# A fused top-k attention and gated feed-forward kernel: weight conversion through one PSUM bank, one rounding moved from ScalarE to GpSimd, GpSimd's budget of tasks 2.25 instead of 2.0

## The chip, the cores and the metric

The kernel runs on one core of a Trainium2 chip. The metric is the device time of one execution in microseconds. Before the change the median of three runs is 1152.47 us (1152.42 to 1154.94).

## The reference

For 8 batches and 8 heads, 576 rows of queries, keys and values of 64 columns: scores, all but the 32 largest of each row masked out, softmax, times the values. The heads side by side are the input x (8, 576, 512) of a feed-forward part: expansion to 1024 columns, relu, a convolution of three taps along the rows, a sigmoid gate, contraction to 512 columns.

```python
scores = scale * np.matmul(q, k.transpose(0, 1, 3, 2))
kth = np.partition(scores, -top_k, axis=-1)[..., -top_k:-top_k + 1]
scores = np.where(scores >= kth, scores, -1000000000.0)
attn = np.exp(scores - max); attn = attn / (sum + 1e-09)
x = np.matmul(attn, v)                       # heads side by side
h = np.maximum(x @ w_in, 0.0)
conv_out += conv_w[k] * hp[:, k:k + S, :]    # k = 0, 1, 2
gate = 1.0 / (1.0 + np.exp(-conv_out))
return (h * gate @ w_out).astype(np.float32)
```

The three weights arrive as 64-bit floats (NumPy's square roots, by which they are scaled, make them so), q, k and v as 32-bit floats.

## The kernel before

The attention is cut into 288 tiles of 128 rows by 576 scores: 32 pairs of heads, nine tiles each. One call of `iteration(it)` issues one step of a software pipeline, in which some eight tiles are in different states. The order in which each engine gets its instructions is the order of this code; the engines themselves run free and wait for each other by semaphores. In an iteration:

- TensorE transposes the masked weights of an old tile, multiplies those of a still older one by the values, computes the scores of a new tile, and in between does feed-forward matmuls, as many as a budget (`FEED`) allows.
- ScalarE, in its order: relu of an expansion, the rounding of gated activations where one is due (L531), the signs ("side", L268), the copy of the scores out of PSUM ("rows", L228), other copies; then the exponential of the scores into PSUM (L280), which waits until the weighing has read the one before, then the tanh of a gate (L465), then its share of a weight block (L155 to L157).
- VectorE: in a loop of seven places, a maximum of a seventh of a tile's row ("cand", L235) in each place, with steps of the search for the 32nd largest of another tile between them, the maximum of the flipped row (L283) in the third place and the selection of the threshold ("hot", L287) in the fifth. Behind the loop come gates (L473), and as the last the weighing (L293): mask times exponential, with the row's sum.
- GpSimd: its share of a weight block (L166 to L172), then the flip ("z", L273: scores times their sides) of one tile, and before or behind it tasks of the feed-forward part from a queue.

The queue of GpSimd, `pool_tasks`, holds planned costs and the earliest iteration of each task. In each iteration `state.pool` gets `POOL_BUDGET`, less 1.5 for a converted block, with deficits carried over. Tasks are issued while more than 0.2 is left. The flip goes in front of the next task as soon as less than `FLIP_AT` = 1.5 is left, and at the end of the iteration at the latest. Tasks are the two halves of a convolution (L439, L448), the three steps of a normalisation (L372 to L374), a gate now and then, and the subtraction (L535) of a rounded activation.

The weight conversion (`class Convert`) is a pipeline of its own over the first iterations: 33 blocks (a small one of the convolution, 16 of 128x256 of each matrix), one an iteration. VectorE masks the exponent field out of a block's high word (`split`, L150, L151), ScalarE makes powers of two and mantissas of it (`act`, L155 to L157), VectorE puts the sign on the power (`sign`, L161), GpSimd multiplies and splits the product into a rounded part and the rest (`pool`). The masks stand in the first places of VectorE's loop, the sign behind the loop. All temporaries lie in SBUF. Feed-forward work starts when the input weights are converted and the first batch's attention is there.

`Contract.split` readies half of a contraction: the gated activations g are rounded to the matmul's format (hi) on ScalarE at once, and the rest g - hi (lo) is a task of GpSimd. Behind the last attention tile (`state.it > NT + 4`) VectorE makes the rest instead.

Of the kernel before, what the change touches and what calls it, by code (L numbers as in the profile page):

```python
# [13 lines left out]
BF16 = mybir.dt.bfloat16  # L14
U16 = mybir.dt.uint16
U32 = mybir.dt.uint32
AF = mybir.ActivationFunctionType
# [21 lines left out]
CB = 1  # L39
BELOW_AT = 2  # L40
NATB = 2
POOL_BUDGET = 2.0
PE_CAP = 1.6
FEED = 1.42
CONV_COST = 1.5
# [18 lines left out]
def attend_and_feed(ctx: ExitStack, tc: tile.TileContext, q, k, v, weights, out, shared, finish=None):  # L64
# [53 lines left out]
    def bank(name):  # L118
        return ps.tile([P, BANK], F32, name=name, tag=name, bufs=1)
# [6 lines left out]
    class Convert:  # L126
# [5 lines left out]
        def load(self):  # L132
            i = Convert.count
            Convert.count += 1
            if not scratch:
                scratch.append(moe.tile([P, 4 * SPB, WB], F32, name="scratch", tag="split"))
            self.at = i % SPB * 4
            tag = ("x_hi", "x_lo")[i % 2]
            self.raw = xp.tile([P, self.src.shape[-1], 2], U32, name="raw64", tag=tag)[0:self.n]
            nc.sync.dma_start(out=self.raw.rearrange("a c t -> a (c t)"), in_=self.src.bitcast(U32))  # L140
# [2 lines left out]
            return scratch[0][0:self.n, self.at + i, 0:self.raw.shape[1]]  # L143

        def split(self):
            exponent, self.mantissa, self.rest = (self.tmp(i) for i in range(3))
            n = exponent.shape[1]
            self.field, self.power = exponent.bitcast(U16)[:, 0:n], exponent.bitcast(BF16)[:, n:2 * n]
            self.top = self.raw.rearrange("a c t -> a (c t)").bitcast(U16).rearrange("a (c t) -> a c t", t=4)[:, :, 3]
            yield lambda: nc.vector.tensor_scalar(self.field, self.top, 0x7FF0, None, ALU.bitwise_and)  # L150
            yield lambda: nc.vector.tensor_scalar(self.mantissa.bitcast(U32), self.raw[:, :, 1], 0xFFFFF, 0x100000,  # L151
                                                  ALU.bitwise_and, ALU.bitwise_or)

        def act(self):
            nc.scalar.activation(out=self.power, in_=self.field, func=AF.Exp, scale=math.log(2.0) / 16, bias=offset)  # L155
            nc.scalar.activation(out=self.mantissa, in_=self.mantissa.bitcast(U32), func=AF.Copy, scale=2.0 ** -20)
            nc.scalar.activation(out=self.rest, in_=self.raw[:, :, 0], func=AF.Copy, scale=2.0 ** -52)  # L157

        def sign(self):
            power = self.power.bitcast(U16)  # L160
            yield lambda: nc.vector.scalar_tensor_tensor(out=power, in0=self.top, scalar=0x8000, in1=power,  # L161
                                                         op0=ALU.bitwise_and, op1=ALU.bitwise_or)

        def pool(self):
            x = self.mantissa
# [330 lines left out]
    class Contract:  # L496
# [11 lines left out]
        def split(self):  # L508
# [18 lines left out]
            state.split += 1  # L527
            state.splits += 0 if late else 1
            state.late_splits += 1 if late else 0
            for a, z, src in srcs:  # L530
                nc.scalar.copy(out=self.hi[:, :, a:z], in_=src)  # L531

            def rest(engine):
                for a, z, src in srcs:
# [1 line left out]
                self.ready = True  # L536
                unready.remove(self)

            if state.it > NT + 4:
                rest(nc.vector)  # L540
            else:
                pool_tasks.append((state.it + 1, 1.3, lambda: rest(nc.gpsimd)))

        def room(self):
# [169 lines left out]
    def iteration(it):  # L714
# [45 lines left out]
        for i in range(max(7, len(a_ops), len(b_ops))):  # L760
            if i < len(a_ops):
                a_ops[i]()
            for op in c_first[i:i + 1]:
                op()
            if tD is not None and not exact:
                if i == BELOW_AT:
                    below(tD)
                if i == BELOW_AT + 2:
                    select(tD)
            if i < len(b_ops):  # L770
                b_ops[i]()
        for op in c_last:
            op()
        while gates:
            gates.popleft().gate()
        recs, rec_next = rec_next, []
# [189 lines left out]
```

## Time and profile before

| | |
|---|---|
| median of 3 runs | 1152.47 us |
| the profiled execution | 1155.28 us |
| its span, first to last instruction | 1153.4 us |
| mean granted TensorE clock | 0.963 of full |
| TensorE busy (matmuls) | 1035.3 us |
| VectorE busy | 1064.5 us |
| ScalarE busy | 996.5 us |
| GpSimd busy | 895.6 us |

Busy times are unions of instruction spans on an engine; DVE is VectorE, ACT is ScalarE, POOL is GpSimd, PE is TensorE and PEld its weight loads. The pipelines of TensorE and VectorE overlap neighbouring instructions a little, so the sums of durations are larger than the busy time. Durations and stretches come from the profiled execution.

### The profile page before, as it was taken

What the parts mean: (1) busy time and instruction counts of PE and PEld (TensorE: products, weight loads), DVE (VectorE), ACT (ScalarE), POOL (GpSimd) and SP (SyncE); (2) the same over time, 40 slices, a digit from 0 to 9 for tenths busy, and PEclk for the clock granted to TensorE, in tenths of its full rate; (3) what the DMA queues carried; (4) which work ended last, traced back from release to release, by engine and by line L of the source; (5) the groups of instructions that cost most, each with busy time, mean ns of one, the idle gap of its engine ahead of it and who ended that gap; (6) DMA issues with size and microseconds to landing.
All of it is one profiled execution on the core that took longest, in us unless ns stands there. A gap on an engine that the chain in (4) does not pass through costs nothing.

```text
span 1153.4 us, 27267 instructions
## 1 busy us (share of the span) xinstructions
PE 1035.3 (90%) x7970; PEld 767.3 (67%) x7970; DVE 1064.5 (92%) x5834; ACT 996.5 (86%) x2343; POOL 895.6 (78%) x1078
## 2 busy tenths in 40 slices
PE   3665676788999999999999999999999999999997
PEld 1443444566767776777777767777777677777896
DVE  7999999999999999999999999999999999998651
ACT  5777868899999999999999999999999999998442
POOL 6788864688979888898978887987978897898300
PEclk9967659999999999999999999999999999999999
DMA  7221101111111111111111112121211011110001
GB/s 242 79 68 41 46 17 40 46 38 44 55 54 56 56 46 65 46 55 56 49 38 44 56 45 64 47 64 46 64 55 56 24 38 59 55 33 21 31 28 40
DMA packets 51694, 60.75 MB, mean 53 GB/s; under 512 B 9776, under 2 KB 30544, under 8 KB 51536
## 3 DMA queue, kind: packets, MB, share of 16 engines
q1 hardware_dynamic: 51536, 58.91, 16.0%
q8 instruction: 66, 1.08, 0.4%
q14 instruction: 92, 0.75, 0.2%
HBM read 49.31 MB, written 9.58 MB: 51 GB/s over the span
## 4 chain that ended last, share of the span: by engine, by line
DVE 45%; PE 42%; ACT 11%; issue 1%; DMA 0%; SPq 0%; POOL 0%; ACTq 0%; POOLq 0%
DVE cand L235 13%; DVE e L293 9%; PE mc L554 9%; PE me L404 8%; DVE z L283 7%; PE s_ps L337 6%; PE s_ps L219 5%; PE pt L306 5%; DVE cand L257 3%; ACT weights_ps L280 2%; DVE scratch L161 2%; DVE rows L255 2%; PE s_ps L222 2%; DVE hot L287 2%; PE weights_ps L554 2%; PE s_ps L214 2%
## 5 line engine op out<-in xcount | busy, mean ns | idle before, releaser
L273 POOL TENSOR_TENSOR z<-rows,side 128x579 f32<-128x579 f32 x288 | 347.4, 1206 | 143.0 <-ACT side L268 122.5
L235 DVE MAX8 cand<-rows 128x8 f32<-128x82 f32 (+1 forms) x2016 | 451.0, 238 | 0.0
L280 ACT ACTIVATE weights_ps<-rows,z 128x576 f32<-128x576 f32 x288 | 219.8, 763 | 42.4 <-DVE e L293 31.5
L293 DVE SCALAR_TENSOR_TENSOR e<-rows,kth,weights_ps 128x576 f32<-128x576 f32 x288 | 230.1, 799 | 0.3
L268 ACT ACTIVATE side<-rows 128x576 bf16<-128x576 f32 x288 | 224.2, 778 | 0.8 <-DVE rows L255 0.5
L404 PE MATMUL me<-x_hi,wi 128*128 128x322 f32 (+1 forms) x928 | 218.6, 308 | 1.2 <-ACT g L418 1.2
L283 DVE MAX8 z<-z 128x8 f32<-128x576 f32 x288 | 213.7, 742 | 0.0
L228 ACT COPY rows<-s_ps 128x576 f32<-128x576 f32 x288 | 183.0, 635 | 33.7 <-PE s_ps L340 20.3
L219 PE MATMUL s_ps<-k,q 64*128 64x512 f32 x512 | 155.1, 684 | 59.6 <-ACT xt L348 44.9
L306 PE MATMUL pt<-ident,e 128*128 128x128 f32 x1152 | 191.8, 292 | 8.9 <-DVE e L293 8.9
L337 PE MATMUL s_ps<-pT,vn 128*64 128x128 f32 (+1 forms) x2560 | 171.2, 279 | 17.7 <-ACT rows L228 17.7
L554 PE MATMUL mc<-wo,split 128*128 128x512 f32 x684 | 186.5, 406 | 0.0
L337 PEld LDWEIGHTS s_ps<-pT,vn 128*64 128x64 f32 x2560 | 134.3, 143 | 54.7 <-ACT rows L228 28.0
L306 PEld LDWEIGHTS pt<-ident,e 128*128 128x128 f32 x1152 | 135.3, 148 | 35.3 <-issue 20.1
L404 PEld LDWEIGHTS me<-x_hi,wi 128*128 128x128 f32 x928 | 157.1, 189 | 2.4 <-ACT g L418 2.1
L311 ACT COPY pT<-pt 128x512 f32<-128x512 f32 x256 | 152.0, 594 | 3.4 <-PE pt L306 3.2
L404 PE MATMUL me<-x_lo,wi 128*128 128x258 f32 (+1 forms) x464 | 138.5, 299 | 0.0
L554 PEld LDWEIGHTS mc<-wo,split 128*128 128x128 f32 x684 | 120.1, 189 | 19.6 <-issue 0.2
L437 POOL TENSOR_SCALAR t<-g,cr 128x256 f32<-128x256 f32 (+1 forms) x222 | 113.6, 512 | 0.0
L222 PEld LDWEIGHTS s_ps<-k,q 128*128 128x128 f32 x256 | 40.9, 201 | 105.6 <-issue 105.6
L255 DVE MAX8 rows<-cand 128x8 f32<-128x21 f32 x576 | 108.9, 189 | 0.2 <-issue 0.2
L219 PEld LDWEIGHTS s_ps<-k,q 64*128 64x128 f32 x512 | 40.6, 194 | 91.2 <-ACT xt L348 58.8
(121 smaller groups left out, 1865.6 us busy)
## 6 DMA issues: line engine op xcount, KB each, us to landing
k<-in_k_dram SPq DMA_DIRECT2D x32, 352.0 KB
q<-in_q_dram SPq DMA_DIRECT2D x32, 288.0 KB
vn<-in_v_main_dram SPq DMA_DIRECT2D x32, 256.0 KB
rb<-row SPq DMA_DIRECT2D x64, 128.0 KB
out_dram<-o SPq DMA_DIRECT2D x24, 256.0 KB
raw<-in_w_in_dram SPq DMA_DIRECT2D x16, 256.0 KB
raw<-in_w_out_dram SPq DMA_DIRECT2D x16, 256.0 KB
vt<-in_v_tail_dram SPq DMA_DIRECT2D x32, 64.0 KB
```

What stands on the lines that cost most here:

```text
L219: nc.tensor.matmul(s_ps[:, 2 * h * BANK:(2 * h + 1) * BANK], lhsT=qx[d, at], rhs=kx[d, h * TAIL:h * TAIL + MAIN], start=True, stop=True)
L228: nc.scalar.copy(out=x, in_=s_ps[:, at:at + S])
L235: yield lambda c=c, at=at, n=n: nc.vector.max(out=t.cand[:, c:8 * CHUNKS:CHUNKS], in_=t.x[:, at:at + n])
L268: nc.scalar.activation(out=t.side[:, 2:S + 2], in_=t.x, func=AF.Sign, scale=-OVER, bias=t.row[:, 7:8], accum_out=t.cnt)
L273: nc.gpsimd.tensor_tensor(t.z[:, 8:S + 11], t.row[:, 6:S + 9], t.side, ALU.mult)
L280: nc.scalar.activation(out=e_ps, in_=t.x, func=AF.Exp, scale=scale, bias=t.shift)
L283: nc.vector.max(out=t.z[:, 0:8], in_=t.z[:, 10:S + 10])
L293: nc.vector.scalar_tensor_tensor(out=t.e, in0=t.x, scalar=kth[:, t.n:t.n + 1], in1=e_ps, op0=ALU.is_ge, op1=ALU.mult, accum_out=t.pc.sums[ ...
L306: nc.tensor.transpose(tp[:, i * P:(i + 1) * P], t.e[:, o + i * P:o + (i + 1) * P], ident)
L337: nc.tensor.matmul(a[r, 0:w], lhsT=st.pc.vn[:, h, i], rhs=st.pT[:, h if st.i < NI else 1 - h, i, 0:w], start=(i == 0), stop=False)
L404: nc.tensor.matmul(mm[:, 0:w], lhsT=wt, rhs=xx, start=(n == 0), stop=(n == len(ops) - 1))
L554: nc.tensor.matmul(mm[0:m], lhsT=x[:, i], rhs=wo[:, e, f], start=start, stop=stop)
```

## The change

Four things change. The exponent field and the mantissa bits of a weight block move from SBUF to two halves of one PSUM bank (that of "mc", which no contraction uses yet), in whole 4-byte words; ScalarE makes the power of two in SBUF and copies it to the field's place, one instruction more, and the sign is put on from there. The sign and the two masks of the next block go to the fifth, sixth and seventh place of VectorE's loop, the sign first. The rounding of gated activations becomes a task of GpSimd, with a planned cost of 0.65, in front of its subtraction; behind the last tile it stays on ScalarE. `POOL_BUDGET` goes from 2.0 to 2.25.

```diff
-POOL_BUDGET = 2.0
+POOL_BUDGET = 2.25
@@ Convert.load
                 scratch.append(moe.tile([P, 4 * SPB, WB], F32, name="scratch", tag="split"))
+                mc = bank("mc")
+                scratch.extend((mc[:, 0:WB], mc[:, WB:2 * WB]))
@@ Convert.split
-            exponent, self.mantissa, self.rest = (self.tmp(i) for i in range(3))
-            n = exponent.shape[1]
-            self.field, self.power = exponent.bitcast(U16)[:, 0:n], exponent.bitcast(BF16)[:, n:2 * n]
-            self.top = self.raw.rearrange("a c t -> a (c t)").bitcast(U16).rearrange("a (c t) -> a c t", t=4)[:, :, 3]
-            yield lambda: nc.vector.tensor_scalar(self.field, self.top, 0x7FF0, None, ALU.bitwise_and)
-            yield lambda: nc.vector.tensor_scalar(self.mantissa.bitcast(U32), self.raw[:, :, 1], 0xFFFFF, 0x100000,
+            self.power, self.mantissa, self.rest = (self.tmp(i) for i in range(3))
+            self.two = self.power.bitcast(BF16)[:, 0:self.power.shape[1]]
+            self.field, self.bits = (x[0:self.n, 0:self.raw.shape[1]] for x in scratch[1:])
+            self.top = self.raw[:, :, 1]
+            yield lambda: nc.vector.tensor_scalar(self.field.bitcast(U32), self.top, 0x7FF00000, None, ALU.bitwise_and)
+            yield lambda: nc.vector.tensor_scalar(self.bits.bitcast(U32), self.top, 0xFFFFF, 0x100000,
                                                   ALU.bitwise_and, ALU.bitwise_or)
@@ Convert.act
-            nc.scalar.activation(out=self.power, in_=self.field, func=AF.Exp, scale=math.log(2.0) / 16, bias=offset)
-            nc.scalar.activation(out=self.mantissa, in_=self.mantissa.bitcast(U32), func=AF.Copy, scale=2.0 ** -20)
+            nc.scalar.activation(out=self.two, in_=self.field.bitcast(U32), func=AF.Exp, scale=math.log(2.0) / 2 ** 20,
+                                 bias=offset)
+            nc.scalar.copy(out=self.field, in_=self.two)
+            nc.scalar.activation(out=self.mantissa, in_=self.bits.bitcast(U32), func=AF.Copy, scale=2.0 ** -20)
@@ Convert.sign
-            power = self.power.bitcast(U16)
-            yield lambda: nc.vector.scalar_tensor_tensor(out=power, in0=self.top, scalar=0x8000, in1=power,
-                                                         op0=ALU.bitwise_and, op1=ALU.bitwise_or)
+            yield lambda: nc.vector.scalar_tensor_tensor(out=self.power.bitcast(U32), in0=self.top, scalar=0x80000000,
+                                                         in1=self.field.bitcast(U32), op0=ALU.bitwise_and,
+                                                         op1=ALU.bitwise_or)
@@ Contract.split
-            for a, z, src in srcs:
-                nc.scalar.copy(out=self.hi[:, :, a:z], in_=src)
+            def cast():
+                for a, z, src in srcs:
+                    if state.it > NT + 4:
+                        nc.scalar.copy(out=self.hi[:, :, a:z], in_=src)
+                    else:
+                        nc.gpsimd.tensor_scalar(self.hi[:, :, a:z], src, 1.0, 0.0, ALU.mult, ALU.add)
...
-            if state.it > NT + 4:
+            if late:
+                cast()
                 rest(nc.vector)
             else:
+                pool_tasks.append((state.it + 1, 0.65, cast))
                 pool_tasks.append((state.it + 1, 1.3, lambda: rest(nc.gpsimd)))
@@ iteration
-            for op in c_first[i:i + 1]:
+            for op in (c_last + c_first)[i - 4:i - 3] if i > 3 else ():
                 op()
...
-        for op in c_last:
-            op()
         while gates:
             gates.popleft().gate()
```

## Rows read from the trace of the kernel before

**Rows 1.** The page, part 1: busy time, share of the span, instructions, by engine.

```profile
PE 1035.3 (90%) x7970; PEld 767.3 (67%) x7970; DVE 1064.5 (92%) x5834; ACT 996.5 (86%) x2343; POOL 895.6 (78%) x1078
```

**Rows 2.** Busy time by stretch: length, busy us (instructions) by engine, clock, DMA.

```profile
20.00:160.00 140.00, 84.78 (x478) 52.76 (x479) 139.79 (x620) 102.95 (x252) 115.91 (x148) 0.77 0.17 53
160.00:180.00 20.00, 16.36 (x106) 10.01 (x108) 16.70 (x102) 15.08 (x35) 10.74 (x12) 0.68 0.21 65
300.00:1000.00 700.00, 683.08 (x5511) 509.55 (x5510) 677.16 (x3937) 663.83 (x1556) 599.06 (x704) 1.00 0.16 51
```

**Rows 3.** Line 293 from 29 to 120 us: count, ns min/median/max, first and last start.

```profile
L293 DVE SCALAR_TENSOR_TENSOR e<-rows,kth,weights_ps x19: 798/801/804, 29.6 to 119.5; 128x576 f32<-128x576 f32 x19
```

**Rows 4.** Groups by line, 20 to 160 us: busy us, mean ns | idle before, releasers.

```profile
L161 DVE SCALAR_TENSOR_TENSOR scratch<-raw,scratch 128x256 uint16<-128x256 uint16 x29 | 29.5, 1018 | 0.0
L150 DVE TENSOR_SCALAR scratch<-raw 128x256 uint16<-128x256 uint16 x27 | 15.7, 582 | 0.0
L151 DVE TENSOR_SCALAR scratch<-raw 128x256 uint32<-128x256 uint32 x27 | 11.6, 429 | 0.0
```

**Rows 5.** Timeline in the head: start us, us, engine line op.

```profile
63.50 1.21 POOL L273 TENSOR_TENSOR z<-rows,side 128x579 f32<-128x579 f32 x1 [1.09 <-ACT side L268]
...
63.73 1.25 DVE L161 SCALAR_TENSOR_TENSOR scratch<-raw,scratch 128x256 uint16<-128x256 uint16 x1
...
71.15 0.27 DVE L150 TENSOR_SCALAR scratch<-raw 128x256 uint16<-128x256 uint16 x1
...
71.58 0.33 DVE L151 TENSOR_SCALAR scratch<-raw 128x256 uint32<-128x256 uint32 x1
...
72.30 0.40 ACT L156 ACTIVATE scratch<-scratch 128x256 f32<-128x256 uint32 x1
...
73.19 0.23 DVE L235 MAX8 cand<-rows 128x8 f32<-128x82 f32 x1
...
73.90 0.40 DVE L161 SCALAR_TENSOR_TENSOR scratch<-raw,scratch 128x256 uint16<-128x256 uint16 x1
```

**Rows 6.** Groups by line, whole span: gates with and without PSUM, and a PSUM write.

```profile
L473 DVE SCALAR_TENSOR_TENSOR g<-weights_ps,g 128x256 f32<-128x256 f32 x49 | 19.9, 407 | 0.0
L473 DVE SCALAR_TENSOR_TENSOR g<-t,g 128x256 f32<-128x256 f32 x8 | 3.3, 423 | 0.8 <-ACT t L465 0.8
L352 DVE TENSOR_SCALAR weights_ps<-sums 128x9 f32<-128x9 f32 x32 | 5.5, 170 | 1.1
```

**Rows 7.** Groups by line, 20 to 160 us: ScalarE’s exponential, GpSimd’s first add.

```profile
L280 ACT ACTIVATE weights_ps<-rows,z 128x576 f32<-128x576 f32 x27 | 20.2, 747 | 32.9 <-DVE e L293 27.4 <-DVE rec L353 3.9 <-DVE cand L235 1.5
L166 POOL TENSOR_TENSOR scratch<-scratch 128x256 f32<-128x256 f32 x28 | 23.9, 854 | 0.0
```

**Rows 8.** Timeline of VectorE behind the last block: two weighings.

```profile
155.15 0.80 DVE L293 SCALAR_TENSOR_TENSOR e<-rows,kth,weights_ps 128x576 f32<-128x576 f32 x1
...
175.25 0.80 DVE L293 SCALAR_TENSOR_TENSOR e<-rows,kth,weights_ps 128x576 f32<-128x576 f32 x1
```

**Rows 9.** Groups by line, 300 to 1000 us: the flip, and hot.

```profile
L273 POOL TENSOR_TENSOR z<-rows,side 128x579 f32<-128x579 f32 x201 | 242.1, 1205 | 84.3 <-ACT side L268 78.4 <-DVE rows L255 3.7 <-POOL split L535 1.0
L287 DVE SCALAR_TENSOR_TENSOR hot<-weights_ps,cnt,z 128x10 f32<-128x10 f32 x201 | 43.2, 215 | 21.1 <-ACT weights_ps L465 16.0 <-ACT weights_ps L280 4.1
```

**Rows 10.** Line 531, the roundings on ScalarE, 200 to 1050 us.

```profile
L531 ACT CAST split<-g x56: 406/622/714, 276.7 to 1046.2; 128x512 fp32r<-128x512 f32 x50, 128x256 fp32r<-128x256 f32 x6
L531 ACT CAST split<-ends x6: 391/404/434, 492.1 to 1014.0; 128x256 fp32r<-128x256 f32 x6
```

**Rows 11.** Lines 373 and 171: roundings of other tiles on GpSimd.

```profile
L373 POOL TENSOR_SCALAR x_hi<-xt x32: 661/672/844, 104.3 to 1080.2; 128x576 fp32r<-128x576 f32 x32
...
L171 POOL TENSOR_SCALAR wi<-scratch x16: 404/404/428, 12.8 to 81.3; 128x256 fp32r<-128x256 f32 x16
```

**Rows 12.** Timeline around 820 us: a flip, and the exponential that reads it.

```profile
819.54 1.20 POOL L273 TENSOR_TENSOR z<-rows,side 128x579 f32<-128x579 f32 x1
...
822.32 0.77 ACT L280 ACTIVATE weights_ps<-rows,z 128x576 f32<-128x576 f32 x1
```

## The prediction

> **What bounds the kernel now.** I read the page's busy line first: VectorE 92%, TensorE 90%, ScalarE 86%, GpSimd 78% of the span [rows 1]. Four engines that full cannot be told apart by a mean, so I split the span into stretches. From 20 to 160 us VectorE is busy 139.79 of 140 us and no other engine is over 83%: this is the head, where the weights are converted, one block to an iteration, and VectorE sets the pace. From 300 to 1000 us TensorE (97.6%) and VectorE (96.7%) are both nearly full, ScalarE stands at 95%, GpSimd at 86% [rows 2]. Behind that comes a tail of feed-forward matmuls, which is TensorE's.
>
> One weighing (L293) ends each iteration, so its starts are a ruler. Nineteen of them run from 29.6 to 119.5 us: 89.9 / 18 = 4.99 us an iteration [rows 3]. In the steady stretch there are 201 iterations in 700 us: 3.48 us each [rows 9]. So the head pays 1.5 us more an iteration, for the 27 blocks that are masked from 20 us on [rows 4], 25 of them at this full pace, and for the ramp before.
>
> What is in that 1.5 us? The three conversion operations on VectorE take 1018, 582 and 429 ns on the mean, 2.03 us together [rows 4]. These means are not work. One sign operation (L161) starts at 63.73, beside a GpSimd multiply that runs from 63.50 to 64.71, and takes 1.25 us; the same operation takes 0.40 at 73.90, and the masks (L150, L151) take 0.27 and 0.33 at 71.15 and 71.58 [rows 5]. So each often waits out a GpSimd operation that got in first. The weighing, one of whose operands lies in PSUM, never does: 798 to 804 ns over all 19 [rows 3].
>
> The Trainium skill says the like in "SBUF — State Buffer", section "Who interferes with whom": VectorE and GpSimd share one pair of SBUF ports, a lock held for a whole instruction, which a VectorE instruction wants if it has two SBUF inputs or runs in a two-port mode. The sign and the weighing agree with the first half; a mask has one input, so by that rule it must run in such a mode, which no row here shows.
>
> **The change, part by part.**
>
> *Head, VectorE.* The sign operation will have one SBUF and one PSUM input, and the masks read 4-byte words and write PSUM. If all three take what they take when nothing is in their way, an iteration loses 1.018 - 0.40 + 0.582 - 0.27 + 0.429 - 0.33 = 1.03 us: 4.99 - 1.03 = 3.96 [rows 3 to 5]. For the price of a PSUM operand the nearest row is the gate (L473) at 128x256: 407 ns with a PSUM input, 423 with all in SBUF; a nine-column tensor_scalar into PSUM takes 170 ns [rows 6], about what is left of 330 ns when 256 columns are taken off at the weighing's slope, 0.8 us for 576. So the three cost 0 to 0.2 us more than the free ones; I take 0.1: 4.06.
>
> "VectorE: DVE Perf Modes" in the Trainium skill, section "The TRN2 errata", speaks against this: a VectorE operation from PSUM has a fixed part of 120 cycles, one from SBUF of 58. For the one PSUM input of a block that is 65 ns, an estimate from that page, and 2 us over the head. The gate's two rows don't bear it out.
>
> *Head, the new wait.* The sign moves from the end of the iteration to its fifth place, and field and bits lie in one bank that ScalarE uses too, so it must wait until ScalarE has done that block's exponential, the new copy and the mantissa. That a bank is guarded as a whole is seen in "hot" (L287): it reads constants, and waits 16.0 us for a ScalarE write to other columns of their bank [rows 9]. In the iteration with the free masks ScalarE's mantissa ends at 72.30 + 0.40 = 72.70; the copy in front of it, of the same shape, adds at most 0.40, some 0.35 with the overlap: 73.05. VectorE comes to the sign behind the fifth chunk, 73.19 + 0.23, and no longer has the two masks ahead of it, -0.60: 72.82 [rows 5]. The wait is 0.2 us (0 to 0.4). Behind it in VectorE's queue stand "hot", two chunks, both masks and the weighing, and ScalarE's next exponential waits for that, so it counts whole: 4.26.
>
> *Head, the other engines.* ScalarE is busy 102.95 of 140 us, 3.67 of each 4.99, with the copy 4.05. It has the room, for it waits 32.9 us for VectorE's weighing [rows 2, 7]. GpSimd is busy 115.91 of 140, 4.13 an iteration; its first add (854 ns [rows 7]) loses a port wait of its own, so some 4.1. TensorE's granted clock is 0.77 there and 0.68 from 160 to 180 us, so part of both is at the lower level, 1.2 GHz [rows 2]. Behind the last block, with no conversion and no feed-forward matmul yet, five iterations take 175.25 - 155.15 = 20.1 us, 4.02 each [rows 8], with TensorE's late results as what holds them. So at 4.26 VectorE still sets the pace, but three others stand at 4.0 to 4.1 and their waits will not all fall together: I take 4.4, bounds 3.96 and 4.75 (the latter if each iteration pays a wait of half a microsecond). Saved: 25 x (4.99 - 4.4) = 15 us (bounds 6 and 26), and 2 (0 to 4) in the ramp. The head is a fixed number of iterations, so what it saves moves everything behind it.
>
> *Steady stretch, ScalarE.* 62 roundings (56 + 6) of 0.62 us, 0.40 for the 12 short ones, leave ScalarE between 276 and 1046 us: 36 us [rows 10]. What can come of it is bounded twice: TensorE idles 16.9 us of 700, and VectorE waits 21.1 of 700 at "hot" [rows 2, 9]. Only those waits can give, and the feed-forward matmuls have to be done whatever the iteration takes. I take 3 us, bounds 0 and 10.
>
> *Steady stretch, GpSimd.* The same rounding takes 404 ns there at 256 columns and 672 at 576 [rows 11], so 0.62 at 512: 50 x 0.62 + 12 x 0.40 = 36 us over some 770. Busy goes from 86 to about 90%, and 78.4 us of waiting for ScalarE's sides in 700 [rows 9] are there to fill. Queued behind a rounding on GpSimd stand its subtraction and that iteration's flip (L273), for which ScalarE's next exponential waits, and VectorE's max behind it. In the tightest iteration from 200 to 1050 us the flip ends at 820.74 and that exponential starts at 822.32: 1.58 us of room [rows 12]; one rounding fits. The larger budget admits 2.25 instead of 2.0 of planned cost to an iteration; what it is spent on is the same work, so it costs nothing unless flips come late. A contraction becomes ready at most an iteration later, and TensorE has expansions to put in its place. I take 0, bounds -2 and +10.
>
> *Tail.* There the rounding stays on ScalarE and the subtraction on VectorE: 0.
>
> **Sum.** -15 - 2 - 3 = -20 us on the profiled execution's 1155.28 (span 1153.4 and 1.9 around it): 1135. The median of the runs, 1152.47, is 2.8 lower: forecast 1132.
>
> **Rivals.**
> 1. The head goes to the floor of 3.96 and the freed ScalarE takes away half of the waits at "hot": -26 - 4 - 10 = -40, 1112. For it: "hot" waits for ScalarE alone. Against: three other engines stand at 4.0 to 4.1.
> 2. The bank holds the head up, ScalarE and VectorE each late behind the other, 4.75 an iteration: -6, 1146. For it: "hot" pays for sharing a bank already. The Trainium skill asks for such waits in "PSUM — Partial Sum Buffer", section "PSUM bank collisions raise a hardware error": engines are to be kept apart by bank, not by address. The row of "hot" agrees.
> 3. Slower: GpSimd sets the pace of the steady stretch. The place is the flip behind rounding and subtraction: both are admitted before it, since 2.25 - 0.65 is still over the flip's mark of 1.5. It decides once the delay exceeds the room, 1.58 us at the tightest. If 62 such groups cost the rounding's 0.6 each: 37 - 20 = +17, 1169. For it: GpSimd at 90%, and a budget that with a flip fills 3.5 us. Against: its 78.4 us of waiting, and only one rounding to two or three iterations.
> 4. It does not do what it says: masks and sign, with one operand still in SBUF, wait for the port as before: -3, 1150.
>
> **How the numbers follow.** Forecast 0.63, rival 1 0.12, rival 2 0.13, rival 3 0.06, rival 4 0.06. About 0.3%, 3.5 us, is what a measurement of this kernel can tell. Faster: 0.63 + 0.12 and 0.10 of rival 2, 0.85; same: the rest of rival 2 and rival 4, 0.09; slower: 0.06. The range for 8 in 10 leaves out rivals 3 and 4 and the far ends of 1 and 2: 1117 to 1148.
>
> **What would show it.** Right: the sign near 0.41 us in every place and both masks near 0.33, whatever GpSimd does; weighings 4.2 to 4.6 us apart in the head; the steady stretch at 3.45 to 3.5; roundings of 0.62 on GpSimd. Wrong: signs that idle over 0.5 us behind ScalarE, flips that end behind the exponential's turn, or a clock in the head that takes another course.

## The result and the profile after

The changed kernel takes 1136.76 us in the median of 4 runs (1134.84 to 1138.28) against 1153.51 in 4 runs of the kernel before on the same chip: 0.985 of it, interval 0.983 to 0.988. That is 16.8 us less; 20 were forecast, and 1132 us. The profiled execution took 1135.4 us, its span is 1133.6.

The page's busy line of the changed kernel, to be laid beside [rows 1]: VectorE 22 us less, ScalarE 12 less, GpSimd 36 more.

```profile
PE 1020.9 (90%) x7970; PEld 757.7 (67%) x7970; DVE 1042.4 (92%) x5831; ACT 984.1 (87%) x2312; POOL 931.4 (82%) x1147
```

Its stretches (length, busy us of PE, PEld, DVE, ACT and POOL with instructions, granted clock, DMA), which answer to [rows 2]: the head, the iterations right behind it, the steady stretch, and all behind the last weighing.

```profile
20.00:140.00 120.00, 73.49 (x452) 43.98 (x451) 113.12 (x590) 110.25 (x271) 104.70 (x139) 0.81 0.19 62
143.00:170.00 27.00, 18.82 (x166) 12.18 (x164) 26.74 (x163) 24.18 (x57) 19.94 (x21) 0.93 0.15 48
300.00:1000.00 700.00, 687.40 (x5568) 514.01 (x5567) 681.66 (x3958) 648.22 (x1515) 635.96 (x773) 1.00 0.17 52
1045.20:1134.00 88.80, 76.69 (x446) 65.81 (x445) 39.96 (x82) 31.55 (x72) 17.85 (x22) 0.96 0.10 32
```

In the head VectorE is no longer the only full engine: 113.1 of 120 us, with ScalarE at 110.3. In the steady stretch ScalarE went from 663.8 to 648.2 and GpSimd from 599.1 to 636.0, while TensorE and VectorE are each busy some 4 us longer in the same 700. For the stretch behind the head and the one behind the last weighing, the same two rows of the kernel before:

```profile
155.10:180.00 24.90, 19.33 (x127) 12.24 (x125) 21.53 (x127) 18.81 (x44) 15.39 (x17) 0.64 0.17 52
1063.70:1154.00 90.30, 81.69 (x491) 71.48 (x487) 41.30 (x85) 33.87 (x76) 14.40 (x17) 0.97 0.09 31
```

The ruler in the head, the weighing (now L297), which answers to [rows 3]:

```profile
L297 DVE SCALAR_TENSOR_TENSOR e<-rows,kth,weights_ps x19: 797/802/808, 28.6 to 110.5; 128x576 f32<-128x576 f32 x19
```

Nineteen weighings from 28.6 to 110.5 us: 81.9 / 18 = 4.55 us an iteration on the mean, against 4.99; 12 of the 18 take 4.45. And the three conversion operations on VectorE from 28 to 138 us, which answer to [rows 4] (busy us, mean ns, idle before and its releaser):

```profile
L164 DVE SCALAR_TENSOR_TENSOR scratch<-raw,mc 128x256 uint32<-128x256 uint32 x24 | 10.1, 422 | 6.1 <-ACT scratch L160 6.1
L152 DVE TENSOR_SCALAR mc<-raw 128x256 uint32<-128x256 uint32 x25 | 10.4, 415 | 0.0
L153 DVE TENSOR_SCALAR mc<-raw 128x256 uint32<-128x256 uint32 x25 | 10.4, 415 | 0.0
```

Every one of them has a constant duration now (the signs 420 to 423 ns, the masks 410 to 420), though every sign starts while a GpSimd operation runs, and 1.25 us in sum replace 2.03. In front of the sign (L164) stands the new wait, 6.1 us in 24 iterations, for ScalarE's mantissa (L160). One iteration of the timeline (start us, us, engine, line) shows it:

```profile
94.67 0.38 ACT L160 ACTIVATE scratch<-mc 128x256 f32<-128x256 uint32 x1
...
95.08 0.42 DVE L164 SCALAR_TENSOR_TENSOR scratch<-raw,mc 128x256 uint32<-128x256 uint32 x1 [0.19 <-ACT scratch L160]
...
95.84 0.41 DVE L152 TENSOR_SCALAR mc<-raw 128x256 uint32<-128x256 uint32 x1
...
96.32 0.41 DVE L153 TENSOR_SCALAR mc<-raw 128x256 uint32<-128x256 uint32 x1
...
96.64 0.80 DVE L297 SCALAR_TENSOR_TENSOR e<-rows,kth,weights_ps 128x576 f32<-128x576 f32 x1
```

Mantissa, 0.19 us of idle, sign, masks, and from the sign's start to the weighing's 1.56 us. The steady stretch's flip and "hot", which answer to [rows 9], and the roundings on GpSimd, which answer to [rows 10]:

```profile
L277 POOL TENSOR_TENSOR z<-rows,side 128x579 f32<-128x579 f32 x202 | 243.4, 1205 | 44.3 <-ACT side L272 37.0 <-PE pt L310 4.5 <-PE s_ps L226 2.2
...
L291 DVE SCALAR_TENSOR_TENSOR hot<-weights_ps,cnt,z 128x10 f32<-128x10 f32 x202 | 43.5, 215 | 16.7 <-ACT weights_ps L469 14.6 <-ACT weights_ps L284 1.2
```

```profile
L540 POOL TENSOR_SCALAR split<-g x57: 404/619/631, 265.2 to 1041.5; 128x512 fp32r<-128x512 f32 x51, 128x256 fp32r<-128x256 f32 x6
...
L540 POOL TENSOR_SCALAR split<-ends x6: 404/406/423, 482.1 to 989.1; 128x256 fp32r<-128x256 f32 x6
```

GpSimd's wait for sides halves, 78.4 to 37.0 us; VectorE's at "hot" goes from 21.1 to 16.7.

Where the 19.8 us of span went, with the starts of the first, 28th, 55th and last weighing as marks: up to the 28th (162.2 before, 149.6 after) 12.6 us, all in the ramp and the head; from there to the 55th (253.7 and 237.8) 3.3; from the 55th to the last (1063.7 and 1045.2) 2.6; from the last to the last matmul's end (1145.7 and 1123.9) 3.3; and the last copies and outputs took 2.0 us longer than before. The second of these need not be the kernel's: behind the head the granted clock was 0.64 in the one execution and 0.93 in the other, as the two rows show, and that differs between executions of the same instructions too (last section).

### The profile page after: what moved, and what is told of

Read it like the earlier page. It is cut to its first block, busy times and chain, and to the rows that moved or that the text cites. A ratio compares the mean times of both kernels' runs of the same rounds, so it can differ in the third digit from the quotient of the medians.

```text
span 1133.6 us, 27377 instructions
## 1 busy us (share of the span) xinstructions
PE 1020.9 (90%) x7970; PEld 757.7 (67%) x7970; DVE 1042.4 (92%) x5831; ACT 984.1 (87%) x2312; POOL 931.4 (82%) x1147
## 4 chain that ended last, share of the span: by engine, by line
PE 52%; DVE 34%; ACT 11%; issue 2%; DMA 0%; POOL 0%; SPq 0%; ACTq 0%
PE me L408 11%; PE mc L565 10%; DVE cand L239 9%; DVE e L297 8%; PE s_ps L341 7%; PE s_ps L223 7%; PE pt L310 6%; DVE z L287 5%; ACT weights_ps L284 3%; PE s_ps L226 3%; DVE cand L261 2%; DVE hot L291 2%; PE weights_ps L565 2%; PE s_ps L218 2%; DVE rows L259 2%
## 5 line engine op out<-in xcount | busy, mean ns | idle before, releaser
L239 DVE MAX8 cand<-rows 128x8 f32<-128x82 f32 (+1 forms) x2016 | 456.2, 239 | 0.1
L297 DVE SCALAR_TENSOR_TENSOR e<-rows,kth,weights_ps 128x576 f32<-128x576 f32 x288 | 230.5, 800 | 0.1
L310 PE MATMUL pt<-ident,e 128*128 128x128 f32 x1152 | 188.4, 288 | 2.9 <-DVE e L297 1.8
L565 PE MATMUL mc<-wo,split 128*128 128x512 f32 x696 | 190.1, 406 | 0.0
L341 PE MATMUL s_ps<-pT,vn 128*64 128x128 f32 (+1 forms) x2560 | 167.3, 275 | 17.4 <-ACT rows L232 17.4
L341 PEld LDWEIGHTS s_ps<-pT,vn 128*64 128x64 f32 x2560 | 131.1, 140 | 55.7 <-ACT rows L232 27.2
L310 PEld LDWEIGHTS pt<-ident,e 128*128 128x128 f32 x1152 | 132.4, 145 | 28.5 <-issue 14.8
L565 PEld LDWEIGHTS mc<-wo,split 128*128 128x128 f32 x696 | 122.2, 189 | 19.8 <-issue 0.2
```

Source lines behind the costliest of these rows:

```text
L239: yield lambda c=c, at=at, n=n: nc.vector.max(out=t.cand[:, c:8 * CHUNKS:CHUNKS], in_=t.x[:, at:at + n])
L297: nc.vector.scalar_tensor_tensor(out=t.e, in0=t.x, scalar=kth[:, t.n:t.n + 1], in1=e_ps, op0=ALU.is_ge, op1=ALU.mult, accum_out=t.pc.sums[ ...
L310: nc.tensor.transpose(tp[:, i * P:(i + 1) * P], t.e[:, o + i * P:o + (i + 1) * P], ident)
L341: nc.tensor.matmul(a[r, 0:w], lhsT=st.pc.vn[:, h, i], rhs=st.pT[:, h if st.i < NI else 1 - h, i, 0:w], start=(i == 0), stop=False)
L565: nc.tensor.matmul(mm[0:m], lhsT=x[:, i], rhs=wo[:, e, f], start=start, stop=stop)
```

## The experiments

Ratios are to runs of the kernel before on the same chip, with 95% intervals. Experiments 1 to 4 and 12 ran on one chip, 5 to 8 on another, 9 to 11 on a third; from chip to chip the ratios are what can be compared. Edits are against the changed kernel unless another is named.

**1. The conversion alone** (PSUM bank and order; rounding on ScalarE, budget 2.0).

```diff
-POOL_BUDGET = 2.25
+POOL_BUDGET = 2.0
...
+            for a, z, src in srcs:
+                nc.scalar.copy(out=self.hi[:, :, a:z], in_=src)
...
-                pool_tasks.append((state.it + 1, 0.65, cast))
```

> Only the weight conversion is changed (PSUM bank, order in VectorE's loop); the rounding stays on ScalarE and the budget at 2.0. My theory: nearly all of the gain is the head, so about 16 us of the 17 come back: 1137 to 1139 against 1153.5; weighings in the head 4.45 us apart as in the whole change. Rival: the moved rounding and the budget make a good part of the gain (half of it or more): 1145 or above.

Measured: 1142.26 us, 0.989 (0.9865 to 0.9914). Some 12 of the 17 us: less than expected, and between the ranges of the two theories. The undisturbed head iterations take 4.45 us as said (4.53 on the mean).

**2. Rounding and budget alone**, with the old conversion in its old order; against the kernel before:

```diff
-POOL_BUDGET = 2.0
+POOL_BUDGET = 2.25
...
+                    if state.it > NT + 4:
+                        nc.scalar.copy(out=self.hi[:, :, a:z], in_=src)
+                    else:
+                        nc.gpsimd.tensor_scalar(self.hi[:, :, a:z], src, 1.0, 0.0, ALU.mult, ALU.add)
...
+                pool_tasks.append((state.it + 1, 0.65, cast))
```

> The old conversion, with the rounding on GpSimd and the budget at 2.25. My theory: the head stays at 4.99 us an iteration, the steady stretch gives 0 to 4 us: 1149.5 to 1153.5. Rival (GpSimd sets the pace of the steady stretch): slower than 1153.5. Rival (the freed ScalarE gives most): 1145 or below.

Measured: 1150.69 us, 0.9971 (0.9951 to 0.9991). 3 to 4 us less, as the theory had it, with head iterations of 4.98 us. The sign still waits, as this row of its head shows:

```profile
L161 DVE SCALAR_TENSOR_TENSOR scratch<-raw,scratch 128x256 uint16<-128x256 uint16 x23 | 22.1, 962 | 0.0
```

**3. The whole change with the old budget.**

```diff
-POOL_BUDGET = 2.25
+POOL_BUDGET = 2.0
```

> The whole change with the budget left at 2.0. My theory: the budget decides only how early GpSimd's tasks are issued, not how much there is; GpSimd's tasks need 1.9 of planned cost an iteration on the mean, so 2.0 still suffices: within 2 us of the whole change, 1135 to 1139. Rival (the budget is what makes room for the moved rounding): tasks fall behind, contractions become ready late, more is left for the tail: 1142 or above.

Measured: 1147.2 us, 0.9937 (0.9916 to 0.9958). My theory fell: without the larger budget the moved rounding is a loss of 5 us against experiment 1, while rounding and budget together (the whole change) are a gain of 4 to 5. The output of this run is not right (a relative error of 0.11), for a cause that the traces don't show; it issues as many matmuls as the others (7970), so its time tells of the schedule and not of a kernel that could be used. The attention is not what gets longer; its last weighing starts at 1043.1 us, 2.1 before that of the whole change. What gets longer is what is left behind it:

```profile
1043.10:1144.00 100.90, 92.13 (x551) 81.09 (x551) 47.05 (x95) 38.15 (x85) 14.34 (x19) 0.98 0.10 31
```

TensorE is busy 92.1 us there against 76.7 in the whole change and 81.7 before; 478 feed-forward matmuls are left, against 397 and 420.

**4. Sign and masks behind the loop.**

```diff
-            for op in (c_last + c_first)[i - 4:i - 3] if i > 3 else ():
-                op()
...
+        for op in c_last + c_first:
+            op()
         while gates:
             gates.popleft().gate()
```

> The whole change, but sign and masks stand behind VectorE's loop instead of in its fifth to seventh place. My theory: the sign's wait of 0.25 us for ScalarE in each of 25 iterations goes, and the head's iterations come down from 4.45 to 4.2 to 4.3 us, where ScalarE (4.09 us busy an iteration) and GpSimd stop them: 4 to 6 us faster than the whole change, 1131 to 1133. Rival (ScalarE sets the head's pace already, the sign's wait is only where it shows): no change, 1136 to 1138, and the wait turns up elsewhere on VectorE.

Measured: 1135.42 us, 0.9836 (0.9811 to 0.986), 1 to 3 us below the whole change, from which the intervals don't part it. The wait is gone but for 0.6 us in 24, and most iterations still take 4.41 us, with VectorE full. The timeline shows where the wait's time went:

```profile
93.95 0.41 DVE L164 SCALAR_TENSOR_TENSOR scratch<-raw,mc 128x256 uint32<-128x256 uint32 x1
...
94.39 0.43 DVE L152 TENSOR_SCALAR mc<-raw 128x256 uint32<-128x256 uint32 x1
...
94.86 0.43 DVE L153 TENSOR_SCALAR mc<-raw 128x256 uint32<-128x256 uint32 x1
...
95.19 0.80 DVE L297 SCALAR_TENSOR_TENSOR e<-rows,kth,weights_ps 128x576 f32<-128x576 f32 x1
```

Start to start, sign, mask and mask take 0.44, 0.47 and 0.33 us; apart, with a chunk between, they took 0.34, 0.33 and 0.32 (in the whole change: 95.84 to 96.17, where the next chunk starts, for the mask). Neither theory had that. The groups from 28 to 138 us show a little idle time in front of the masks, where the whole change has none:

```profile
L153 DVE TENSOR_SCALAR mc<-raw 128x256 uint32<-128x256 uint32 x25 | 10.7, 428 | 0.9
L152 DVE TENSOR_SCALAR mc<-raw 128x256 uint32<-128x256 uint32 x24 | 10.3, 428 | 0.8
```

In the trace each mask waits for a semaphore of VectorE's own, which the operation in front raises, and starts 0.035 us behind that operation's end: sign and masks all touch the one bank, and this fits a program that guards it on its own engine too. The weighing behind them waits for none of VectorE's own and overlaps the second mask. Apart, the masks wait for the same semaphore and lose nothing.

**5. The sign from SBUF.**

```diff
-            self.two = self.power.bitcast(BF16)[:, 0:self.power.shape[1]]
+            self.two = self.tmp(3).bitcast(BF16)[:, 0:self.power.shape[1]]
...
-            nc.scalar.copy(out=self.field, in_=self.two)
+            nc.scalar.copy(out=self.power, in_=self.two)
...
-                                                         in1=self.field.bitcast(U32), op0=ALU.bitwise_and,
+                                                         in1=self.power.bitcast(U32), op0=ALU.bitwise_and,
```

> The whole change, but ScalarE's copy of the power goes to SBUF instead of the PSUM bank, and the sign reads it there: 4-byte words, two SBUF inputs. My theory (a VectorE operation with two SBUF inputs waits out GpSimd's operations): the sign takes 0.42 where GpSimd is idle and 0.6 to 1.0 us on the mean, the head's iterations 4.6 to 4.9 us: 4 to 10 us slower than the whole change, 1141 to 1147. Rival (the 16-bit strided form waited, not the place of the operands): the sign stays near 0.42 everywhere, and as it no longer reads the bank its wait for ScalarE's mantissa goes too: 4.2 to 4.4 us an iteration, 1131 to 1137.

Measured: 1132.42 us, 0.9786 (0.975 to 0.9823), against 0.985 for the whole change. The expected loss did not come. But the rival's reason is not right either: with 4-byte words and two SBUF inputs the sign waits when GpSimd is first, as at 93.92, and makes GpSimd wait when it is first itself, as at 89.77 (two starts of a sign, L164, and the GpSimd operation beside each):

```profile
89.77 0.40 DVE L164 SCALAR_TENSOR_TENSOR scratch<-raw,scratch 128x256 uint32<-128x256 uint32 x1
...
89.83 0.91 POOL L174 TENSOR_TENSOR scratch<-scratch 128x256 f32<-128x256 f32 x1
...
93.82 0.74 POOL L170 TENSOR_TENSOR scratch<-scratch 128x256 f32<-128x256 f32 x1
...
93.92 0.91 DVE L164 SCALAR_TENSOR_TENSOR scratch<-raw,scratch 128x256 uint32<-128x256 uint32 x1
```

0.91 us behind a running add, 0.40 in front of a multiply that then takes 0.91. Ten of 26 signs from 28 to 140 us took over 0.5 us; before, 19 of 23 did. So the wait is real, and what changed is who comes first: the place of the sign in the iteration.

**6. The masks to SBUF.**

```diff
-            self.field, self.bits = (x[0:self.n, 0:self.raw.shape[1]] for x in scratch[1:])
+            self.field = scratch[1][0:self.n, 0:self.raw.shape[1]]
+            self.bits, self.mask = self.mantissa, self.tmp(3)
...
-            yield lambda: nc.vector.tensor_scalar(self.field.bitcast(U32), self.top, 0x7FF00000, None, ALU.bitwise_and)
+            yield lambda: nc.vector.tensor_scalar(self.mask.bitcast(U32), self.top, 0x7FF00000, None, ALU.bitwise_and)
...
```

> The whole change, but both masks write SBUF and ScalarE reads them there; only the power that the sign reads stays in the bank. My theory: a mask of 4-byte words in SBUF has one input and takes 0.33 us, with short waits as L151 had before (0.43 on the mean), against 0.415 into PSUM; the sign then waits for the copy alone, 0.38 us earlier, so its wait goes: 4.15 to 4.3 us an iteration, 4 to 7 us faster than the whole change, 1130 to 1133. Rival (any mask from SBUF to SBUF pays the port as the 16-bit one did, 0.55 to 0.6): 4.4 to 4.6 us, 1136 to 1140.

Measured: 1131.55 us, 0.9788 (0.9757 to 0.982). The time is the theory's, but it comes from a mixture: the quietest iterations take 3.96 us, others up to 5.3, 4.40 on the mean of 18. The masks' rows (ns min/median/max):

```profile
L153 DVE TENSOR_SCALAR scratch<-raw x25: 266/277/803, 30.5 to 136.8; 128x256 uint32<-128x256 uint32 x25
...
L154 DVE TENSOR_SCALAR scratch<-raw x25: 270/337/1191, 30.8 to 137.7; 128x256 uint32<-128x256 uint32 x25
```

**7. The budget of 2.25 with the rounding left on ScalarE.**

```diff
+            for a, z, src in srcs:
+                nc.scalar.copy(out=self.hi[:, :, a:z], in_=src)
...
-                pool_tasks.append((state.it + 1, 0.65, cast))
```

> The whole change, but the rounding stays on ScalarE: conversion and budget 2.25. My theory now: with the rounding gone from GpSimd the larger budget issues convolutions and subtractions earlier, and fewer than 407 feed-forward matmuls (211 contraction, 196 expansion) are left behind the last weighing, so the tail is as short as in the whole change or shorter, while ScalarE's part costs a microsecond or two: 1136 to 1140. Rival (the 4 us come from the freed ScalarE): 1141 to 1143, as with the conversion alone, and some 430 matmuls are left.

Measured: 1140.25 us, 0.9865 (0.9837 to 0.9892), between experiment 1 and the whole change, and their intervals overlap. The tail is the whole change's (76.9 us of TensorE against 76.7), with the last weighing 5.3 us later:

```profile
1050.50:1138.00 87.50, 76.93 (x451) 66.64 (x449) 37.76 (x81) 32.36 (x74) 15.57 (x19) 0.96 0.10 33
```

(The 407 matmuls of the expectation are 397 in the trace of the whole change; some had been counted twice. Here 402 are left.)

**8. Later and apart.**

```diff
+            for op in (c_last + c_first)[i - 5:i - 4] if i > 4 else ():
+                op()
             if i < len(a_ops):
                 a_ops[i]()
-            for op in (c_last + c_first)[i - 4:i - 3] if i > 3 else ():
-                op()
...
+        for op in (c_last + c_first)[2:]:
+            op()
```

> The whole change, but sign and masks stand one place later in VectorE's loop and in front of the chunks: the sign before the sixth, the first mask before the seventh, the second behind it. My theory: behind the loop the wait of 0.25 us went, but three conversion operations in a row took 0.44, 0.46 and 0.34 us start to start instead of 0.33, 0.33 and 0.32, which gave it back. Later and apart, neither is paid: 4.15 to 4.25 us an iteration, 4 to 6 us faster than the whole change, 1131 to 1133. Rival (ScalarE, 4.09 us busy an iteration, sets the pace by its chain): 4.4 us or more with VectorE idle, 1135 to 1138.

Measured: 1128.46 us, 0.976 (0.9733 to 0.9787), faster than either theory had it. Undisturbed iterations take 4.18 us, the sign hardly waits any more (from 28 to 138 us), and VectorE and ScalarE are nearly full in the head:

```profile
L164 DVE SCALAR_TENSOR_TENSOR scratch<-raw,mc 128x256 uint32<-128x256 uint32 x25 | 10.5, 421 | 1.6 <-ACT scratch L160 1.5
```

```profile
20.00:140.00 120.00, 75.41 (x480) 47.13 (x478) 117.98 (x621) 115.76 (x286) 109.56 (x145) 0.84 0.19 62
```

**9. The new order without the PSUM bank** (the kernel before, with rounding on GpSimd and budget 2.25 as in experiment 2, and this edit).

```diff
-            for op in c_first[i:i + 1]:
+            for op in (c_last + c_first)[i - 4:i - 3] if i > 3 else ():
                 op()
...
-        for op in c_last:
-            op()
```

> The old conversion (16-bit forms, all in SBUF, no copy on ScalarE) with only the new order in VectorE's loop, and with rounding and budget as in the whole change. My theory, after the sign from SBUF at its new place waited only 10 times of 26: moving the sign away from the flip, behind which it stood 19 times of 23, gives most of the head's gain, the PSUM operands only the rest: 4.3 to 4.7 us an iteration, 1136 to 1144. Rival (the PSUM bank is what takes the waits away): 4.8 to 5.0 us, 1147 to 1151.

Measured: 1129.6 us, 0.9784 (0.9761 to 0.9806). Faster than either theory had it, and faster than the whole change, beside it on the same chip (experiment 11). Undisturbed iterations take 4.11 us, 4.32 on the mean. Its conversion operations, all SBUF to SBUF in the old forms:

```profile
L161 DVE SCALAR_TENSOR_TENSOR scratch<-raw,scratch 128x256 uint16<-128x256 uint16 x25 | 12.9, 516 | 0.4 <-ACT scratch L155 0.4
...
L151 DVE TENSOR_SCALAR scratch<-raw 128x256 uint32<-128x256 uint32 x25 | 12.3, 491 | 0.0
...
L150 DVE TENSOR_SCALAR scratch<-raw 128x256 uint16<-128x256 uint16 x25 | 8.0, 320 | 0.0
```

1.33 us in sum, against 2.03 before and 1.25 in the whole change, which has a wait of 0.25 and one more ScalarE operation beside them.

**10. Experiment 8 with a budget of 2.5** (the edit is against experiment 8).

```diff
-POOL_BUDGET = 2.25
+POOL_BUDGET = 2.5
```

> Sign and masks later and apart, with a budget of 2.5. My theory: at 2.25 the tasks no longer fall behind, so a larger budget leaves as many feed-forward matmuls to the tail (about 409): within 2 us of that kernel at 2.25 (0.976 of before). Rival (more budget, shorter tail): the tail loses another 3 us, 0.973 or below. Rival (flips come late): slower, 0.979 or above.

Measured: 1132.6 us, 0.9799 (0.9778 to 0.982). It doesn't help. It looks like the second rival's loss, but the interval overlaps that of experiment 8, and a part of the profiled loss falls behind the head at a granted clock of 0.76 against 0.94. Waits for a late flip are there (us, times, longest), 6.8 us together against 1.8 in experiment 8:

```profile
ACT weights_ps L284 <- POOL z L277: 4.6, 10, 0.7
...
DVE z L287 <- POOL z L277: 2.2, 5, 0.8
```

**11. The whole change again**, without an edit.

> The whole change once more, beside the others: 0.985 of before, weighings 4.45 us apart in the head, 407 matmuls behind the last weighing.

Measured: 1138.38 us, 0.9846 (0.9819 to 0.9872).

**12. The order alone**, on the kernel before, with the edit of experiment 9 and nothing else.

> The kernel before with nothing but the new order of sign and masks in VectorE's loop; conversion, rounding and budget as before. My theory now: the order alone takes the port waits away, and rounding and budget add their 4 us on their own: the head as in the run with the order, the rounding and the budget (4.1 us where nothing disturbs it), 1132 to 1136, faster than the whole change. Rival (the order needs the rounding or the budget on GpSimd, which shift its operations against VectorE's): 4.5 us or more, 1142 or above.

Measured: 1134.26 us, 0.9811 (0.9785 to 0.9837). Its ruler, and two GpSimd flips with what VectorE and GpSimd convert between them:

```profile
L293 DVE SCALAR_TENSOR_TENSOR e<-rows,kth,weights_ps x19: 794/796/802, 27.5 to 105.3; 128x576 f32<-128x576 f32 x19
```

```profile
87.78 1.20 POOL L273 TENSOR_TENSOR z<-rows,side 128x579 f32<-128x579 f32 x1
...
88.94 0.73 POOL L166 TENSOR_TENSOR scratch<-scratch 128x256 f32<-128x256 f32 x1
...
89.69 0.41 DVE L161 SCALAR_TENSOR_TENSOR scratch<-raw,scratch 128x256 uint16<-128x256 uint16 x1
...
89.75 0.88 POOL L170 TENSOR_TENSOR scratch<-scratch 128x256 f32<-128x256 f32 x1
...
90.44 0.34 DVE L150 TENSOR_SCALAR scratch<-raw 128x256 uint16<-128x256 uint16 x1
...
90.72 0.41 POOL L171 TENSOR_SCALAR wo<-scratch 128x256 fp32r<-128x256 f32 x1
...
90.86 0.41 DVE L151 TENSOR_SCALAR scratch<-raw 128x256 uint32<-128x256 uint32 x1
...
91.19 0.80 DVE L293 SCALAR_TENSOR_TENSOR e<-rows,kth,weights_ps 128x576 f32<-128x576 f32 x1
...
91.90 1.21 POOL L273 TENSOR_TENSOR z<-rows,side 128x579 f32<-128x579 f32 x1
```

In the kernel before, the sign came behind a flip that was running [rows 5], in 24 of the 29 blocks from 20 to 160 us. Here it starts at 89.69, as an add ends and in front of the multiply (89.75), which waits for it (0.88 us); the masks come beside the end of that multiply and beside the short rounding (L171), and no conversion operation is left for the flip to meet. The waits are not gone but short: the first mask ends 0.15 us behind the multiply, the second 0.14 behind the rounding, and 7 of 25 signs still take over 0.5 us. No instruction, operand or buffer is different: the order alone takes the head from 4.99 to (105.3 - 27.5) / 18 = 4.32 us. From the 28th weighing (143.5 us, 162.2 before) to the last matmul its stretches last what they did before, within 0.8 us each.

## Why the prediction was right, and where it was not

**The time and the stage: right, the sum in part by luck.** The head was to give 17 us (15 and 2 in the ramp); it gave 12.6 to its end. What it lacks was made up by terms that the sum did not have: 3.3 in the tail and 3.3 right behind the head, where the clock took another course, less 2.0 at the end. So 19.8 us of the profiled pair stand against the 20 of the sum.

An iteration took 4.55 us where 4.4 was taken. The working had sign and masks at 1.00 free and 0.1 more for PSUM; they take 1.25, 0.15 more. Its wait of 0.2 (measured 0.25) was right, and it counts whole: 3.96 + 0.25 + 0.25 = 4.46, and the undisturbed iterations take 4.45. The mis-sized term is the masks' PSUM output, 0.415 each. The row that was to show it to be cheap does not: at the weighing's slope 256 columns are 0.36 us, more than all of the 330 ns from which they were taken off, so 170 ns for nine columns are not what is left.

**The cause in the head: half right.** In the changed kernel the PSUM operands do take the waits away. The step that failed is the one behind it: the whole gain was put down to them ("if all three take what they take when nothing is in their way"), and they were not needed. The order does more without PSUM: alone it gives 1.9% (experiment 12), while order and PSUM bank together give 1.1% (experiment 1). With rounding and budget added, 2.2% (experiment 9) against 1.5%. Both pairs, each on one chip, say that the bank costs some 0.6 to 0.8%, 8 to 9 us between the medians. Of these 5 to 6 show in the head of the profiled executions: the 28th weighing starts at 143.5 and 143.6 us without the bank, at 149.0 and 149.3 with it (experiments 12, 9, 1 and 11). Sign and masks cost as much in either form, 1.25 us with the bank and 1.33 with the short waits (experiment 9); what the bank adds is the sign's wait for ScalarE, 0.25 of the 4.55 us. Experiment 8 agrees: its sign waits 1.6 us in all instead of 6.1, and its 28th weighing starts at 142.8. The bank in the old order was not run, so what it gives by itself is not shown.

The prediction priced the move of the sign only as a source of a wait, and did not ask beside which GpSimd operation the old and the new place lie. The rows for that were there: the flip 0.23 us ahead of the sign [rows 5].

**The port: right, and wider than read.** Two SBUF inputs wait at 16 bits [rows 5] and at 32 (experiment 5, 0.40 to 0.95 us); with one PSUM input the sign takes 422 ns over 24. The masks take 410 to 420 ns into PSUM and 0.27 to 1.19 us in SBUF (experiment 6). The working's masks "when nothing is in their way" had something in their way: at 71.15 the multiply runs until 71.27 and the mask ends 0.15 us behind it, at 71.58 the rounding runs until 71.77 and the mask ends 0.14 behind it.

```profile
70.60 0.67 POOL L170 TENSOR_TENSOR scratch<-scratch 128x256 f32<-128x256 f32 x1
...
71.36 0.41 POOL L171 TENSOR_SCALAR wi<-scratch 128x256 fp32r<-128x256 f32 x1
```

All 36 masks from 28 to 120 us of the kernel before end 0.14 to 0.15 us behind the GpSimd operation beside which they start. So a mask's time is set by what is left of that operation, and this is what a new order changes.

The Trainium skill has this in "SBUF — State Buffer", section "Who interferes with whom": an operation of the masks' kind can run in a two-port mode and then contends with GpSimd, and the order of issue decides who is blocked. The waits agree with it; no run shows the mode itself. The dearer PSUM operand that the Trainium skill states in "VectorE: DVE Perf Modes", section "The TRN2 errata", did not show where the working weighed it, at an input: 0.42 against 0.40 us for the sign. PSUM costs more at the masks' output, 0.415 against 0.27 to 0.28 in SBUF with no GpSimd operation in the way (experiment 6).

**ScalarE and GpSimd in the steady stretch: right.** 3 us were taken for ScalarE, and the stretch between the 55th and the last weighing gave 2.6; with the old conversion it gave 2.5 (experiment 2: 250.8 to 1058.3 us). It is the rounding that gives it: with the larger budget and the rounding left on ScalarE the stretch lasts 811.5 us, against 810.0 before and 807.4 in the whole change (experiment 7). 36 us of rounding on GpSimd came as worked out, 0.62 us each, and the flips stayed early enough.

**The budget and the tail: wrong.** The budget was held to cost or give nothing, and the tail was put at 0. The tail gave 3.3 us, and without the budget the moved rounding loses what it saves and 5 us more (experiment 3, with its output not right). A budget in which the tasks only just fit leaves more feed-forward matmuls behind the last weighing (478 against 397), where no attention work hides them. Experiment 7 gives the budget the tail and leaves the rounding the steady stretch.

**Rivals.** The first (the floor of 3.96 us, 1112) did not come: VectorE's own 4.46 stood in front of it, with ScalarE at 4.14 and GpSimd at 3.98 busy us an iteration near where the working had them. The second (the bank holds the head up) was nearest to what is wrong with the change, at 4.55 us and not 4.75. The third needed flips that are late; from 145 to 1000 us the exponential waits 1.2 us for them in the whole change, and 4.6 with a budget of 2.5. The fourth did not happen.

**The better versions.** Old conversion in the new order with rounding and budget (0.978), and the PSUM conversion one place later and apart (0.976) both beat the changed kernel (0.985); between the two the intervals don't decide.

## What to carry to other kernels

When an operation waits for a port that another engine holds, look first at what runs beside it and move it: an order may shorten the wait for nothing, where another memory takes it away at the price of a copy, dearer writes and a wait for the guarded bank. A duration counts as free only when nothing that could hold it runs beside it. When work moves to a queue with a planned budget, raise the budget by what is moved and check what is left at the end: the loss shows there and not where the work went. Test a change of several parts with each part alone, also when the sum comes out as predicted.

## What the runs showed of the hardware

- Of VectorE's conversion operations, those with all operands in SBUF that start beside a GpSimd operation wait for its end: masks end 0.14 to 0.15 us behind it (all 36 from 28 to 120 us of the kernel before), signs with two SBUF inputs 0.28 (16 of 19 there; the other three started first). When VectorE is first, GpSimd waits: its multiply takes 0.88 in front of a sign that started 0.06 us earlier (experiment 12), 0.67 without.
- The same mask of 256 4-byte words took 266 to 277 ns from SBUF to SBUF when undisturbed, and 410 to 420 into PSUM (experiment 6, the whole change).
- Sign and masks start 0.44 and 0.47 us after one another in a row, 0.33 apart with a chunk between (experiment 4). In a row each mask waits for a semaphore that the operation in front raises and starts 0.035 us behind its end; the chunk behind a mask and the weighing start 0.08 to 0.1 us before the one in front has ended.
- TensorE's granted clock right behind the head differs between executions: from 143 to 170 us 0.93 and 0.94 in two traces of the whole change, and 0.81 in experiment 7, which issues the same instructions on every engine up to 260 us. The 27 iterations behind the 28th weighing took 88.2, 88.2 and 90.5 us in them, 91.5 before. Runs of one kernel lie up to 8 us apart (1151.96 to 1159.77 in 23 runs of the kernel before), so a difference of 3 us needs several runs.

```profile
143.00:170.00 27.00, 19.02 (x143) 11.99 (x140) 24.58 (x148) 22.80 (x54) 18.38 (x20) 0.81 0.15 48
```
